# A longer planned landing for the two transfers of a range test, in a list-scheduled recurrence and FFN kernel

## The chip, the core and the metric

The kernel runs on one core of a Trainium2 chip. Its engines are TensorE (PE: matrix products, with its weight loads listed as PEld), VectorE (DVE), ScalarE (ACT), GpSimd (POOL) and SyncE (SP, which here does nothing but issue DMA transfers). Each engine works through its own list of instructions, and semaphores order one engine against another. The metric is the device time of one execution in microseconds; the figure for a kernel is the median of several executions.

## The reference, cut to what matters

A gated linear recurrence (48 channels per head, 8 heads, 4 sequences of 768 steps) is followed by a multiplicative feed-forward network (FFN) on the 3072 resulting rows.

```python
# attention block: q, k, v, f_logit are (4, 8, 768, 48), fp32
f = 1.0 / (1.0 + np.exp(-f_logit))
for t in range(S):
    state = f[:, :, t, :, None] * state + einsum('bhd,bhe->bhde', k[:, :, t], v[:, :, t])
    y[:, :, t] = einsum('bhd,bhde->bhe', q[:, :, t], state)
x = y.transpose(0, 2, 1, 3).reshape(3072, 384)

# FFN: w1, w2 are (384, 1024), w3 is (1024, 1024), w_out is (1024, 384)
a = x @ w1
b = x @ w2
h = a * b @ w3
out = h @ w_out
```

## The kernel before: the parts that matter here

**Two paths and a test between them.** The recurrence is cut into 24 units of 128 steps (`u` = 0 to 23). A fast path (`ranged`) multiplies q by the running product of the gates and k by its inverse. This holds only while these running products stay within a range, so the kernel tests the range at run time; if it is left anywhere, a second path (`general`) computes everything anew. The fast path leaves a flag `left`, and the branch at the very end reads it. On these inputs the second path isn't entered in the profile.

The test needs the last unit's results. It has six small VectorE operations (`judge`), a transfer that writes 112 numbers from SBUF to a scratch buffer in HBM (`told`), a transfer that reads them back as one row of one partition (`heard`), and two more VectorE operations: the row's minimum and the comparison that makes the flag (`decided`).

```python
def judge():
    ...
    nc.vector.tensor_reduce(out=low, in_=lasts, axis=AX.XY, op=ALU.min)             # L1233
    nc.vector.tensor_scalar(zero, ysum, 0.0, None, ALU.mult)                        # L1235
    nc.vector.tensor_reduce(out=nil, in_=zero, axis=AX.X, op=ALU.add)               # L1237
    nc.vector.tensor_scalar(nil, nil, 0.0, None, ALU.is_equal)                      # L1238
    nc.vector.tensor_scalar(low, low, RANGE, None, ALU.is_ge)                       # L1240
    nc.vector.tensor_tensor(good, low, nil, ALU.mult)                               # L1241
def told():
    where["all"] = dram.tile([R, 1], F32, name="good")                              # R = 112
    nc.sync.dma_start(where["all"], where["good"])                                  # L1246
def heard():
    row = work.tile([1, R], F32, name="row")
    nc.sync.dma_start(row, where["all"].rearrange("r one -> one r"))                # L1250
def decided():
    nc.vector.tensor_reduce(out=least, in_=where["row"], axis=AX.X, op=ALU.min)     # L1255
    nc.vector.tensor_scalar(left, least, 0.5, None, ALU.is_lt)                      # L1256
```

**A plan makes the order.** The kernel isn't written in the order in which it is emitted. Every piece of work is a task with an engine, an assumed cost, the tasks it depends on and a priority. `Plan.order()` runs a small list scheduler in Python when the kernel is built: it takes, again and again, the task that can start first by the assumed costs, and the tasks are then emitted in the order of their assumed start. The assumed costs are thus nowhere in the program; only the order on each engine comes from them. A transfer is two tasks, an issue on SP and a task on an engine called "DMA", whose `lag` is the time that a dependent task on another engine must keep from its end:

```python
def after(t, ds):                         # when may task t start, with the tasks ds before it
    return max([0.0] + [d["end"] + (d["lag"] + t["slack"] if d["eng"] != t["eng"] else 0.0) for d in ds])

def moves(n, size, rate, emit, deps, prio, late=0.0):
    for j in range(n):
        i = plan.add("SP", 0.45, (lambda: None) if j else emit, [d] if j else deps, prio - j * 1e-3, takes=["lane"], lag=0.6)
        d = i
        t = plan.add("DMA", size / n / rate, lambda: None, [i], prio - j * 1e-3, lag=1.3 + late, frees=[i])
    return t
```

**The FFN of a block of 512 rows.** Each of the six blocks (`n` = 0 to 5) has two stages. The first makes `a * b` (the tile `ab`); the second, `down(i)`, multiplies it by `wc`, which is w3 @ w_out folded into one matrix. Except in parts of the first two blocks' first stage, both stages use a scheme of 7 products in place of 8, which needs sums ahead of the products and after them. `down` runs twice for each block; its products on PE and its sums on VectorE are as follows (X, Y and Z are PSUM banks, all named `f` in the profile):

```python
m1 : X  = ab(0,0) wc         # PE, L714     k1 : dns["m1"] = X            # ACT, L959
m6 : Y  = abs_[1] wct        # PE, L714     u2 : dns["u2"] = Y + m1       # DVE, L965
m2 : X += ab(0,1) wc         # PE, L714     c11: o1 = X                   # ACT, L972
m7 : Y += abs_[2] wct        # PE, L714     u3 : dns["u3"] = Y + m1       # DVE, L978
m5 : Z  = abs_[0] wct        # PE, L714     c22: o2 = Z + u3              # DVE, L989
m4 : Y += ab(1,1) wct        # PE, L714     c21: o2 = Y + m1              # DVE, L995
m3 : Z += abs_[3] wc         # PE, L714     c12: o1 = Z + u2              # DVE, L1003
S0 to S3: the sums abs_[0] to abs_[3] of parts of ab                      # DVE, L950
...
pe("m7", m7, [q["u2"], q["S2"]], -3)
dve("u3", 0.36, u3, [q["m7"]] + old("c22"))
pe("m4", m4, [q["u3"]], -4)
...
pe("m3", m3, [q["c22"], q["S3"], q["m4"]] + ([judged] if final else []), -4)
```

`u3` reads the bank Y before `m4` adds to it, so `m4` must wait for `u3`. Only the last `down` of the last block needs the test's outcome (`judged`). Each of these matmuls in the source shows as two MATMUL instructions in the profile, so each of m1 to m7 is 8 of them. The first stage of a block uses lines L817 to L856, its sums of x L784; the output rows are stored by L1008, two stores for each `down`.

**Where the test is put in:**

```python
if u == NU - 1:
    looked = plan.add("DVE", 1.0, judge, [tk[i]["y"] for i in range(NU)], -20)
    sent = moves(1, 0.4, 250, told, [looked], 0)
    judged = plan.add("DVE", 0.2, decided, [moves(1, 0.4, 250, heard, [sent], 0)], -20)
```

Of the kernel before, what the change touches and what calls it, by code (L numbers as in the profile page):

```python
# [152 lines left out]
@with_exitstack  # L153
def kernel(
    ctx: ExitStack,
    tc: tile.TileContext,
    q: bass.AP,
    k: bass.AP,
    f_logit: bass.AP,
    v: bass.AP,  # L160
    w1: bass.AP,
    w2: bass.AP,
    w3: bass.AP,
    w_out: bass.AP,
    leaf_mask: bass.AP,
    out: bass.AP,
):
    nc = tc.nc
    const = ctx.enter_context(tc.tile_pool(name="const", bufs=1))
    ident = const.tile([P, P], F32, name="ident")  # L170
    w12 = const.tile([P, 2, KM, DFF], F32, name="w12")
    wc = const.tile([P, KF, DM], F32, name="wc")
    left = const.tile([1, 1], I32, name="left")
    with tc.manual_schedule():
        outside = ranged(tc, q, k, f_logit, v, w1, w2, w3, w_out, out, ident, w12, wc, left)
        with tc.If(outside > 0, preferred_fallthrough_block=True, label="general"):
            general(tc, q, k, f_logit, v, leaf_mask, out, ident, w12, wc)
# [29 lines left out]
def ranged(ctx, tc, q, k, f_logit, v, w1, w2, w3, w_out, out, ident, w12, wc, left):  # L207
# [53 lines left out]
    plan = Plan()  # L261
# [71 lines left out]
# [8 lines that stand above are left out]
# [231 lines left out]
    def together(u):  # L572
        return u >= LOOSE

    def begin(u):

        def emit():
            pairs(u)
            if u % NCH < NCH - 1:
                turn(u)  # L580

        t = tk[u]
        t["a"] = t["t"] = plan.add(
            "PE", 1.5, emit, [t["q"], t["k"]] + past(u, 1, "m", "d", "y") + past(u, 2, "d"), need(u) - 999, slack=0.8,
        )
        paired(u)
# [672 lines left out]
    for u in range(NU):  # L1259
        if u <= NPE:  # L1260
            front(u)
        if u >= NPE:
            if not (u > NPE and together(u - 1)):
                begin(u)
            if u + 1 < NU:
                front(u + 1)
        rest(u)
        if u == NPE - 1:
            weights()
        if u == NU - 1:  # L1270
            looked = plan.add("DVE", 1.0, judge, [tk[i]["y"] for i in range(NU)], -20)
            sent = moves(1, 0.4, 250, told, [looked], 0)
            judged = plan.add("DVE", 0.2, decided, [moves(1, 0.4, 250, heard, [sent], 0)], -20)
        if u % UB == UB - 1:
            ffn(u // UB)
    ready_at = 0.0
# [346 lines left out]
```

## Time and profile before

| what | value |
|---|---|
| time, median of 3 executions (lowest, highest) | 495.4 us (494.01, 496.9) |
| time of the profiled execution, its span | 496.72 us, 495.0 us |
| mean granted TensorE clock over the span | 0.993 of full speed |
| PE busy | 481.2 us |
| VectorE busy | 360.3 us |
| transfer of the 112 numbers to HBM (issue to landing) | 6.2 us |

Times in a profile are counted from the start of its span, in us. "Busy" adds up the instructions of an engine. The clock row of a page gives the clock that TensorE was granted, in tenths of full speed, for each of 40 slices of 12.4 us. A line of the timeline has start, duration, engine, source line, operation, the tiles written and read (out<-in), shapes and the number of merged instructions; what stands in square brackets is how long the engine had been idle before and what ended it. PE's matmuls overlap in their pipeline, so the time that one costs in a dense run is the distance from start to start, and not its duration.

### The profile page before, as it was taken

How to read it: one execution, taken by the hardware profiler on the slowest of the kernel's cores; microseconds unless marked ns; L12 is line 12 of the kernel's file. 1: busy time of each engine (PE TensorE's matmuls, PEld its weight loads, DVE VectorE, ACT ScalarE, POOL GpSimd, SP SyncE). 2: the span in 40 equal slices, each digit the busy share in tenths (PEclk: the TensorE clock that was granted, in tenths of full speed). 3: DMA queues.
4: the chain of work that ended last, by engine and by line, in shares of the span. 5: the costliest groups of instructions: out<-in, count | busy, mean ns of one | idle time of the engine just before them, and what ended most of it. 6: DMA issues, size and time to landing. Idle time of an engine off the chain costs nothing.

```text
span 495.0 us, 9560 instructions
## 1 busy us (share of the span) xinstructions
PE 481.2 (97%) x3696; PEld 411.4 (83%) x3696; DVE 360.3 (73%) x721; ACT 166.1 (34%) x380; POOL 61.6 (12%) x115
## 2 busy tenths in 40 slices
PE   8899999999999999999999999899999999999995
PEld 6788645666799888899888888898899888889994
DVE  7999899989997688698968864256673667664541
ACT  4688446663343553436244431010100111110010
POOL 9210000313211121123211210000000000000000
PEclk9999999999999999999999999799999999999999
DMA  6889476653336563455632111000021000000011
GB/s 175 298 304 267 123 260 246 197 168 81 84 98 176 143 150 91 112 132 153 181 80 53 33 52 47 32 33 0 2 64 49 16 1 0 1 1 0 33 59 45
DMA packets 44920, 50.00 MB, mean 101 GB/s; under 512 B 15426, under 2 KB 34370, under 8 KB 43842
## 3 DMA queue, kind: packets, MB, share of 16 engines
q1 hardware_dynamic: 44866, 49.30, 34.0%
q8 instruction: 31, 0.51, 0.4%
q14 instruction: 23, 0.19, 0.1%
HBM read 40.63 MB, written 8.65 MB: 100 GB/s over the span
## 4 chain that ended last, share of the span: by engine, by line
PE 82%; DVE 7%; DMA 3%; issue 1%; SPq 0%; DVEq 0%
PE f L714 67%; PE f L1176 4%; PE py L490 4%; PE pa L456 2%; PE py L509 2%; PE py L468 2%; DVE place L1208 1%; DMA good<-good 1%; PE f L523 1%; DMA xt<-yt 1%; DVE place L1123 1%; DVE place L1129 1%; DVE bwd L415 1%; PE f L692 1%; DMA row<-good 1%
## 5 line engine op out<-in xcount | busy, mean ns | idle before, releaser
L714 PE MATMUL f<-xt,w 128*128 128x256 f32 (+1 forms) x600 | 159.0, 396 | 0.0
L714 PEld LDWEIGHTS f<-xt,w 128*128 128x128 f32 x600 | 113.5, 190 | 24.7 <-issue 10.8
L714 PE MATMUL f<-place 128*128 128x192 f32 (+1 forms) x504 | 112.1, 350 | 0.4 <-DVE place L950 0.4
L714 PEld LDWEIGHTS f<-place 128*128 128x128 f32 x504 | 87.8, 190 | 6.4 <-DVE place L950 0.7
L549 POOL TENSOR_SCALAR_AFFINE_SELECT A<-A 64x256 f32<-64x256 f32 (+1 forms) x84 | 49.2, 606 | 231.9 <-PE py L468 105.9
L1176 PE MATMUL f<-place 128*128 128x384 f32 x128 | 42.6, 489 | 0.5 <-DVE place L1129 0.5
L817 ACT COPY a<-f 128x256 f32<-128x256 f32 x36 | 13.4, 373 | 81.4 <-PE f L714 69.4
L1176 PEld LDWEIGHTS f<-place 128*128 128x128 f32 x128 | 23.9, 190 | 17.3 <-DVE place L1129 1.1
L714 PE MATMUL f<-xt,place 128*128 128x256 f32 x144 | 37.1, 380 | 0.0
L714 PE MATMUL f<-wc,ab 128*128 128x192 f32 x192 | 35.4, 328 | 0.0
L714 PEld LDWEIGHTS f<-wc,ab 128*128 128x128 f32 x192 | 32.5, 192 | 0.4
L393 DVE TENSOR_TENSOR_SCAN fwd<-gate,floor 112x512 f32<-112x512 f32 x24 | 29.9, 1244 | 2.5 <-ACT gate L385 2.0
L543 ACT COPY A<-pa 64x256 f32<-64x256 f32 (+1 forms) x60 | 24.3, 439 | 20.2 <-PE pa L456 19.6
L415 DVE TENSOR_TENSOR_SCAN bwd<-gate,back 112x512 f32<-112x512 f32 x24 | 29.6, 1232 | 0.7
L714 PEld LDWEIGHTS f<-xt,place 128*128 128x128 f32 x144 | 26.6, 189 | 3.5 <-issue 0.2
L841 DVE TENSOR_TENSOR place<-f,a 128x256 f32<-128x256 f32 x36 | 15.2, 421 | 18.7 <-PE f L714 18.5
L653 ACT COPY sb<-S 48x192 f32<-48x192 f32 x40 | 14.0, 350 | 27.7 <-DVE S L644 18.2
L490 PEld LDWEIGHTS py<-A,vt 128*64 128x64 f32 (+1 forms) x320 | 17.5, 129 | 6.7 <-issue 6.2
L1112 ACT ACTIVATE place<-place 128x512 f32<-128x512 f32 (+2 forms) x24 | 21.4, 893 | 4.0 <-DVE w L1129 2.0
L714 PE MATMUL f<-place,ab 128*128 128x192 f32 x96 | 19.2, 346 | 3.6 <-DVE place L978 3.6
L490 PE MATMUL py<-A,vt 128*64 128x128 f32 x320 | 22.6, 281 | 0.0
L1115 ACT ACTIVATE place<-place 128x512 f32<-128x512 uint32 (+2 forms) x24 | 21.4, 900 | 0.9 <-DMA place<-in_w_out_dram 0.9
(119 smaller groups left out, 641.8 us busy)
## 6 DMA issues: line engine op xcount, KB each, us to landing
place<-in_w_dram SPq DMA_DIRECT2D x8, 1024.0 KB, 4.9
place<-in_w_dram SPq DMA_DIRECT2D x12, 512.0 KB, 9.9
out_dram<-o SPq DMA_DIRECT2D x24, 192.0 KB, 1.9
q<-in_q_dram SPq DMA_DIRECT2D x46, 96.0 KB, 2.5
f<-in_f_logit_dram SPq DMA_DIRECT2D x44, 96.0 KB, 2.4
k<-in_k_dram SPq DMA_DIRECT2D x44, 96.0 KB, 2.3
yt<-ys SPq DMA_DIRECT2D x40, 96.0 KB, 2.1
xt<-yt SPq DMA_DIRECT2D x20, 192.0 KB, 2.7
```

The lines of the kernel that those rows point to most:

```text
L393: nc.vector.tensor_tensor_scan(s["P"], gate[u % 2][:, 0:NQ], floor, 0.0, ALU.mult, ALU.max)
L415: nc.vector.tensor_tensor_scan(s["R"][:, ::-1], gate[u % 2][:, NQ:0:-1], back[:, ::-1], 0.0, ALU.mult, ALU.max)
L490: nc.tensor.matmul(y_block(u, b)[64 * half : 64 * half + w], lhsT=s["v"][:, h * D : h * D + w], rhs=s["A"][:, par, hp], start=zone not in ...
L543: nc.scalar.copy(parts_of(s["A"].rearrange("p r h c -> p (r h c)"))[p0:p1, :, f], parts_of(s["pa"].rearrange("p r n -> p (r n)"))[p0:p1, : ...
L549: nc.gpsimd.affine_select(out=a, in_=a, pattern=pattern, compare_op=ALU.is_ge, fill=0.0, base=0, channel_multiplier=-1,)
L653: nc.scalar.copy(sb[u % 2][rows(par), :, 64 * par : 64 * par + D], s["S"][rows(par)])
L714: nc.tensor.matmul(out_, lhsT=lhs[i], rhs=rhs[i], start=start and i == 0, stop=i == len(lhs) - 1, skip_group_check=True,)
L817: nc.scalar.copy(q["a"], q["X"])
L841: nc.vector.tensor_tensor(ups["u3", k], q["Y"], q["a"], ALU.add)
L1112: nc.scalar.activation(m, hi.bitcast(F32), AF.Abs)
L1115: nc.scalar.activation(lo.bitcast(F32), lo, AF.Copy, bias=2.0, scale=2.0**-51)
L1176: nc.tensor.matmul(w3s["p", jc], lhsT=w3s[jc][:, kc * P : kc * P + P], rhs=wos[:, kc], start=(kc == 0), stop=(kc == KF - 1),)
```

## The change

The two transfers of the test get a further argument, `late` = 20.0. In the plan, a task that depends on either of them on another engine must now keep 21.3 us from its end in place of 1.3. No operation is added or taken away, and no dependency is changed; what changes is the place of the minimum in VectorE's order (behind sums of the FFN that stood behind it), and the place of the second transfer in SP's.

```diff
         if u == NU - 1:
             looked = plan.add("DVE", 1.0, judge, [tk[i]["y"] for i in range(NU)], -20)
-            sent = moves(1, 0.4, 250, told, [looked], 0)
-            judged = plan.add("DVE", 0.2, decided, [moves(1, 0.4, 250, heard, [sent], 0)], -20)
+            sent = moves(1, 0.4, 250, told, [looked], 0, 20.0)
+            judged = plan.add("DVE", 0.2, decided, [moves(1, 0.4, 250, heard, [sent], 0, 20.0)], -20)
```

## The prediction

> **What bounds the kernel now.** I read the page first: the engines' totals and the clock row.
>
> ```profile
> PE 481.2 (97%) x3696; PEld 411.4 (83%) x3696; DVE 360.3 (73%) x721; ACT 166.1 (34%) x380; POOL 61.6 (12%) x115
> ...
> PEclk9999999999999999999999999799999999999999
> ```
>
> PE is busy for 97% of the span, so nearly everything that another engine does is hidden, and only what makes PE stand still, or run slower, counts. The clock row has one bad slice, the 26th, which covers 309.4 to 321.8 us. That is where the test of the range stands. So I went to the chain that ended last, in order of time, around that place:
>
> ```profile
> 301.84 6.17 DMA good<-good
> 308.02 2.61 DMA row<-good
> ...
> 311.40 174.77 PE f L714 x890
> ```
>
> The chain is PE nearly all the way, but here it leaves PE for 9 us and goes through the test's two transfers. From 311.40 on it is matmuls without a break for 174.77 us, so whatever PE gains before 311.40 should reach the end whole. The timeline of these microseconds shows how a test that nobody needs before the end of the kernel gets into PE's way:
>
> ```profile
> 305.65 0.69 DVE L950 TENSOR_TENSOR place<-ab 128x512 f32<-128x512 f32 x1 [0.94 <-PE f L714]
> 306.38 0.69 DVE L950 TENSOR_TENSOR place<-place,ab 128x512 f32<-128x512 f32 x1
> ...
> 306.75 1.46 PE L714 MATMUL f<-wc,ab 128*128 128x192 f32 x8
> 308.02 0.28 SPq L1250 DMA_DIRECT2D row<-good  x1
> 310.65 0.26 DVE L1255 TENSOR_REDUCE least<-row 1x1 f32<-1x112 f32 x1 [3.58 <-DMA row<-good]
> 310.94 0.14 DVE L1256 TENSOR_SCALAR left<-least 1x1 int32<-1x1 f32 x1
> 311.01 0.34 DVE L978 TENSOR_TENSOR place<-f,place 128x192 f32<-128x192 f32 x1
> ...
> 311.40 2.92 PE L714 MATMUL f<-place,ab 128*128 128x192 f32 x8 [3.19 <-DVE place L978]
> ```
>
> VectorE finishes two sums at 307.07 and then stands for 3.58 us in front of the minimum, because the row is still in flight. Behind the minimum stands u3 (L978), which has nothing to do with the test; PE's m4 waits for u3 and starts at 311.40. The windows of the trace (PE, PEld, DVE, ACT and POOL busy, then granted clock, DMA share, GB/s) show a second cost, in the clock column:
>
> ```profile
> 311.40:313.00 1.60, 1.60 (x5) 1.60 (x6) 0.94 (x2) 0.00 (x0) 0.00 (x0) 0.50 0.02 5
> ...
> 316.00:317.00 1.00, 1.00 (x4) 1.00 (x4) 0.07 (x1) 0.00 (x0) 0.00 (x0) 0.50 0.18 63
> 317.00:318.00 1.00, 1.00 (x7) 1.00 (x7) 0.88 (x2) 0.00 (x0) 0.00 (x0) 0.86 0.00 0
> ```
>
> After the pause PE runs at half clock until about 317.3: some 4 matmuls to the microsecond, where there are 7 or 8 later. To size it I took the same three groups of products (m4, m3, and m2 of the other half) once here and once at the last `down`, where the clock is full:
>
> ```profile
> 316.68 1.76 PE L714 MATMUL f<-wc,ab 128*128 128x192 f32 x8
> ...
> 318.28 4.06 PE L714 MATMUL f<-place 128*128 128x192 f32 x24
> ```
>
> ```profile
> 478.19 1.46 PE L714 MATMUL f<-place,ab 128*128 128x192 f32 x8
> ...
> 482.09 4.06 PE L714 MATMUL f<-place 128*128 128x192 f32 x24
> ```
>
> From the start of m4 to the start of the next products it is 318.28 - 311.40 = 6.88 us here and 482.09 - 478.19 = 3.90 us there, for the same 24 matmuls.
>
> **What the Trainium skill says.** "TensorE: Matmul & The Clock Gate", its opening table: VectorE's and ScalarE's queues are strictly first in, first out. The trace agrees: u3's bank was complete at about 306.9, VectorE sat idle, and u3 still ran only after the minimum. The same page, Part 1 (The HAM clock gate): after an idle window of about 3.4 us the array's clock is halved, and it takes a busy window to bring it back; the windows run freely, so the outcome depends on how a pause falls on them. The trace agrees: a pause of 3.19 us, then a clock of 0.50 for about 6 us. "Perfetto Trace Analysis", DMA Instruction — HWDGE: the final semaphore write waits until the data is written, which can take surprisingly long when the target is HBM. Here 0.4 KB to HBM took 6.17 us. "DMA: Bandwidth & Descriptors", Rules for kernel authors: issue the transfer early, and wait on its semaphore late. That is this change.
>
> **The change part by part.** The order of instructions of both kernels, engine by engine, differs in two places only. On VectorE the minimum and the comparison leave their place ahead of u3 and go 53 instructions further back, into the first stage of the next block, behind an L838. On SP the second transfer goes behind the four stores of this block's two `down`s. PE's, ScalarE's and GpSimd's orders stay.
>
> *The gap.* The 8 matmuls at 306.75 take 1.30 us start to start at full clock (as 478.19 to 479.49 for a group of 8), so m4 could start at 306.75 + 1.30 = 308.05. It starts at 311.40. With the minimum gone, u3 needs the end of m7 (302.85 + 4.06 = 306.91 in the timeline) and of VectorE's sum before it (306.38 + 0.69 = 307.07); it takes 0.34, so it ends at about 307.45, 0.6 us ahead of need. The gap goes whole: 311.40 - 308.05 = **3.35 us**.
>
> *The clock.* Without a pause there is no reason for the clock to fall: 6.88 - 3.90 = **2.98 us**.
>
> *What follows directly.* m3 needs c22 (L989, right after u3, done at about 307.85), and m2 of the other half needs k1, which needs c21. At the last `down` the same chain runs at full clock: c21 (L995) starts at 479.69, k1 ends at 480.46, m2 starts at 480.79. So 0.3 us stay free, and no wait replaces the one removed.
>
> *The minimum's new place.* The fourth store waits for an L1003 that now ends at 327.93, and 6.3 us earlier after the change, at 321.6. The second transfer goes out behind that store: 0.34 + 0.28 us for the two issues, and 2.6 us to land, as now; it is there at about 325. The L838 ahead of the new place ends at 353.10 now, at about 346.8 then: the row has some 22 us to spare. The two operations take 0.26 + 0.14 us, about 0.43 with the spaces between, and VectorE is idle there for 0.37 us. They stick out by 0.06 us beside a PE that doesn't wait at that place: 0.
>
> *SP.* The stores no longer stand behind a transfer that waits for another; the next gathers of x (L687) come at 358.6 and wait for PE. 0.
>
> *Sum.* 3.35 + 2.98 = **6.33 us**, all on the path: 1.3% of the span.
>
> **The rivals.**
>
> *The clock's dip isn't the pause's.* If it comes from something else, only the gap goes: 3.35 us, 492 to 493 us. For it: 3.19 us is less than the page's window. Against it: over the rest of the trace the windows show full clock, and the dip begins inside this pause.
>
> *A wait takes its place.* u3 could wait for something else, or the minimum could wait again further back and hold an L852 behind it. The first would leave a part of the 3.35, as at the last `down` (0.45 us of PE's waiting for L978; there no other matmuls stand between m7 and m4, as they do here). The second needs a row over 20 us late. About 490.5 to 491 for the first, 495 for the second.
>
> *The end is set elsewhere.* If the last block waited for its x or for a store, the gain would be given back, and the time would stay at 495. Against it: 174.77 us of unbroken PE, and x of the last block is gathered at 358 to 362 for use beyond that.
>
> *The profiled execution isn't the typical one.* Its 496.72 us is near the top of the three (494.01 to 496.9). The spread of 2.9 us is about as large as the clock's part; and how far the clock falls should depend on where the pause falls in the windows, as should the gap on the write to HBM. Then the median execution has less to lose than 6.33 us. I take this to be partly so.
>
> **From these to the time.** Working from the profiled execution: 496.72 - 6.33 = 490.4. From the median with the whole loss: 495.4 - 6.33 = 489.1. From the median with half the clock's part: 495.4 - 3.35 - 1.5 = 490.55. I choose **490.2 us**, 1.05% less. For 8 in 10 I take 488.6 to 491.8: the low end is the median with the whole loss and 0.5 us of luck, the high end lets most of the clock's part stay or be absent in the typical execution. A gain of over 2% would need 485.5 us, 9.9 us off where the trace holds 6.3: 0.02. Slower by 2% needs a new wait of 10 us, and none is in sight: 0.01.
>
> **What would show it.** In the changed kernel's timeline: u3 (L978) in the middle of this stage right behind the second of the two L950, no wait of PE for it of over 0.1 us, and start to start 3.90 us, not 6.88, for the next 24 matmuls; no 7 in the clock row; L1255 some 35 to 40 us further back than the test's first part, without a wait for the row; the times of executions closer together than 2.9 us. Wrong would be: a dip of the clock without the pause, a PE wait near the minimum's new place, or a stage after 318 us that takes longer than before.

## The result, and the profile after

The changed kernel takes **490.3 us** (median of 4 executions, 489.99 to 490.37) against 495.24 us before (median of 4, 494.01 to 496.9): a ratio of 0.9897, 95% interval 0.9867 to 0.9926. The profiled execution takes 490.37 us with a span of 488.7; before it was 496.72 and 495.0.

The same two rows of the page, engines and granted clock:

```profile
PE 477.4 (98%) x3696; PEld 408.0 (83%) x3696; DVE 359.8 (74%) x721; ACT 166.2 (34%) x380; POOL 61.5 (13%) x115
...
PEclk9999999999999999999999999999999999999999
```

The instruction counts are those of before, and VectorE has lost nothing of its work. The 7 in the clock row is gone. The chain that ended last, around the place where it went through the test's two transfers:

```profile
298.20 1.06 PE py L490 x14
299.26 0.58 PE py L509 x16
299.84 30.26 PE f L714 x165
```

Here it doesn't leave PE any more. The timeline of the same stage, with the two sums on VectorE, PE's group ahead of m4, u3, m4, m3 and the next products:

```profile
305.70 0.69 DVE L950 TENSOR_TENSOR place<-ab 128x512 f32<-128x512 f32 x1 [0.94 <-PE f L714]
306.43 0.69 DVE L950 TENSOR_TENSOR place<-place,ab 128x512 f32<-128x512 f32 x1
...
306.80 1.46 PE L714 MATMUL f<-wc,ab 128*128 128x192 f32 x8
307.04 0.35 DVE L978 TENSOR_TENSOR place<-f,place 128x192 f32<-128x192 f32 x1
...
308.10 1.46 PE L714 MATMUL f<-place,ab 128*128 128x192 f32 x8
309.40 1.46 PE L714 MATMUL f<-wc,place 128*128 128x192 f32 x8
...
312.00 4.06 PE L714 MATMUL f<-place 128*128 128x192 f32 x24
```

u3 (L978) follows the sums at once, and m4 starts at 308.10 with no idle time in brackets. From m4 to the next products it is 312.00 - 308.10 = 3.90 us, at full clock. The test's remains stand further back in the timeline:

```profile
322.14 0.30 SPq L1250 DMA_DIRECT2D row<-good  x1
...
346.40 0.42 DVE L838 TENSOR_TENSOR place<-f,a 128x256 f32<-128x256 f32 x1
346.74 0.25 DVE L1255 TENSOR_REDUCE least<-row 1x1 f32<-1x112 f32 x1
347.02 0.14 DVE L1256 TENSOR_SCALAR left<-least 1x1 int32<-1x1 f32 x1
347.19 0.42 DVE L852 TENSOR_TENSOR ab<-f,a 128x256 f32<-128x256 f32 x1
```

The minimum has no bracket: its row has long landed. And the first transfer was no faster than before: 7.2 us to HBM, where it had been 6.2. It is hidden, not shortened.

### The profile page after: what moved, and what is told of

The parts are those of the page before. It is cut to its first block, busy times and chain, and to the rows that moved or that the text cites. A ratio compares the mean times of both kernels' runs of the same rounds, so it can differ in the third digit from the quotient of the medians.

```text
span 488.7 us, 9559 instructions
## 1 busy us (share of the span) xinstructions
PE 477.4 (98%) x3696; PEld 408.0 (83%) x3696; DVE 359.8 (74%) x721; ACT 166.2 (34%) x380; POOL 61.5 (13%) x115
## 4 chain that ended last, share of the span: by engine, by line
PE 86%; DVE 6%; issue 1%; DVEq 0%
PE f L714 69%; PE f L1176 4%; PE py L490 4%; PE pa L456 2%; PE py L509 2%; PE py L468 2%; DVE place L1208 1%; PE f L523 1%; DVE place L1123 1%; DVE place L1129 1%; DVE bwd L415 1%; PE f L692 1%; DVE fwd L393 1%; DVE place L1222 0%; DVE place L950 0%
## 5 line engine op out<-in xcount | busy, mean ns | idle before, releaser
L1112 ACT ACTIVATE place<-place 128x512 f32<-128x512 f32 (+2 forms) x24 | 21.3, 886 | 4.0 <-DVE w L1129 2.0
L714 PE MATMUL f<-place,w 128*128 128x256 f32 x72 | 21.4, 379 | 0.0
L1115 ACT ACTIVATE place<-place 128x512 f32<-128x512 uint32 (+2 forms) x24 | 21.3, 893 | 0.0
```

The source lines that it names most:

```text
L714: nc.tensor.matmul(out_, lhsT=lhs[i], rhs=rhs[i], start=start and i == 0, stop=i == len(lhs) - 1, skip_group_check=True,)
L1112: nc.scalar.activation(m, hi.bitcast(F32), AF.Abs)
L1115: nc.scalar.activation(lo.bitcast(F32), lo, AF.Copy, bias=2.0, scale=2.0**-51)
```

## The experiments

The theory: VectorE works its queue in order, so a minimum whose row is in flight holds up u3, u3 holds up PE's m4, and PE's pause lowers its clock for the work that follows. The rivals: a part of the gain comes from SP's order; the dip of the clock has another cause; the minimum costs wherever it stands.

**Only the second transfer gets the 20 us.** This leaves SP's order as it was and moves only VectorE's two operations (by 23 instructions; the expectation below says 22).

```diff
-    judged = plan.add("DVE", 0.2, decided, [moves(1, 0.4, 250, heard, [sent], 0)], -20)
+    judged = plan.add("DVE", 0.2, decided, [moves(1, 0.4, 250, heard, [sent], 0, 20.0)], -20)
```

> Only the second transfer (the row's way back) gets the 20 us; the first keeps 1.3. VectorE's minimum then stands 22 instructions further back, and SP's order is that of the kernel before: the row's transfer ahead of the four stores. Theory (only VectorE's place of the minimum counts): 490.3 us within 0.5, no wait of PE for L978 in this stage. Rival (a part of the gain comes from SP, whose stores no longer stand behind a transfer that waits for another): between 491 and 494 us.

Measured: 490.34 us (4 executions, 490.12 to 490.40), ratio to before 0.9927 (0.9900 to 0.9954), and no wait of PE for L978 in this stage. All of the gain is there without SP's new order, so SP has no measurable part in it.

**A step of a few instructions: 1 us.** The edit is that of the run above with 1.0 in place of 20.0. The minimum then stands behind u3, c22 and a sum, ahead of c21.

> The second transfer gets 1.0 us in place of 20. VectorE's minimum then stands behind u3, c22 and one sum, ahead of c21. Theory (a queue in order stands still at the minimum until the row lands, whatever comes behind it): u3 runs at 307.1 and m4 follows without a gap, but c21 has to wait for the row (310.65 in the profile before) plus 0.4 us for the minimum and the comparison; it ends about 311.45 in place of 309.96, k1 about 311.85, and PE waits some 1.2 us ahead of m2 of the other half. The pause is too short to lower the clock: 491.5 us, or up to 492.5 us when the row is a microsecond later. Rival (any step out of u3's way gives all of the gain): 490.3 us. Rival (the wait as such costs, wherever it stands): 495 us.

Measured: 491.14 us (8 executions, 489.83 to 491.77, seven of them above 490.8), ratio 0.9938 (0.9919 to 0.9957). The timeline shows the same standstill one step further on:

```profile
310.40 0.26 DVE L1255 TENSOR_REDUCE least<-row 1x1 f32<-1x112 f32 x1 [2.13 <-DMA row<-good]
...
311.19 0.32 ACT L959 COPY place<-f 128x192 f32<-128x192 f32 x1 [7.87 <-DVE o L995]
...
311.56 1.57 PE L714 MATMUL f<-wc,ab 128*128 128x192 f32 x8 [0.80 <-ACT place L959]
```

VectorE stands 2.13 us in front of the minimum, c21 (L995) waits behind it, ScalarE's k1 (L959) for c21, and PE 0.80 us for k1. The chain is the expected one; its end is 0.3 us earlier than estimated (k1 done at 311.51, not 311.85). A stall of VectorE of 2.13 us makes PE wait for only 0.80 us, because m4 and m3 lie ahead of what it holds up.

**4 us, five instructions back.** Again the same edit, with 4.0: the minimum stands behind c12 (L1003).

> The second transfer gets 4.0 us. The minimum then stands behind u3, c22, a sum, c21 and c12 of the same half: 5 instructions further back than before, where the change puts it 53 further back. Theory (it is enough that the row has landed when VectorE gets to the minimum, or that nothing urgent stands behind it): c12 ends at about 311.3, the row lands at about 310.5, the sum and u2 behind it are needed by PE only at 313 or later: 490.3 us within 0.3. Rival (only a long way back is safe, since the landing varies by a microsecond or two): a median of 490.5 to 491.5 with executions above 491.

```profile
310.86 0.36 DVE L1003 TENSOR_TENSOR o<-f,place 128x192 f32<-128x192 f32 x1 [0.94 <-PE f L714]
311.13 0.25 DVE L1255 TENSOR_REDUCE least<-row 1x1 f32<-1x112 f32 x1
```

Measured: 490.34 us (4 executions, 490.20 to 490.38), ratio 0.9910 (0.9879 to 0.9940). The row has landed by 311.13, the minimum doesn't wait, and five instructions give all that 53 give.

**One transfer inside SBUF, at the old place in the plan.** The numbers go straight from a column over 112 partitions into a row of one partition.

```diff
+def crossed():
+    row = work.tile([1, R], F32, name="row")
+    nc.sync.dma_start(row, where["good"])
+    where["row"] = row
...
-    sent = moves(1, 0.4, 250, told, [looked], 0)
-    judged = plan.add("DVE", 0.2, decided, [moves(1, 0.4, 250, heard, [sent], 0)], -20)
+    judged = plan.add("DVE", 0.2, decided, [moves(1, 0.4, 250, crossed, [looked], 0)], -20)
```

> The plan of the kernel before, but the test's numbers go from one column over 112 partitions to one row of one partition in one transfer inside SBUF, without the scratch buffer in HBM and without the second transfer. The minimum keeps its old place ahead of u3. Theory (the landing of two chained transfers over HBM, 8.8 us, is what VectorE waits for): one transfer inside SBUF lands in about 2 to 2.6 us, at about 304.3, before VectorE gets to the minimum at 307.07; minimum and comparison take 0.43 us, u3 ends at about 307.9, ahead of the 308.05 at which m4 may start: 490.3 to 490.5 us. Rival (the place ahead of u3 is itself costly): over 492 us. Rival (112 elements of 4 bytes are slow wherever they go, 6 us): the row at 308, a gap of about 0.9 us on PE, 491.2 us.

The lines of the timeline: the last operation ahead of the minimum, and the minimum itself.

```profile
304.27 0.36 DVE L965 TENSOR_TENSOR place<-f,place 128x192 f32<-128x192 f32 x1 [1.84 <-PE f L714]
304.54 0.25 DVE L1260 TENSOR_REDUCE least<-row 1x1 f32<-1x112 f32 x1
```

Measured: 490.25 us (4 executions, 490.19 to 490.29), ratio 0.9926 (0.9899 to 0.9954). The transfer lands 1.9 us after its issue. With one transfer in place of two the plan put the minimum two instructions earlier than I had said, ahead of the two sums, and it still doesn't wait there. So an early place costs nothing by itself; what cost was the row in flight. It is also a second way to the same time: the answer comes sooner, where the change has VectorE ask for it later.

**PE kept busy in the pause: first at the wrong place.** To part the clock from the gap, seven matmuls into a bank that nobody reads were put on PE ahead of an m4 (14 MATMUL instructions in the profile). The first try chose a later block:

```diff
 def m4():
+    if n == NB - 2 and i == 0:
+        spare = ps.tile([P, 2, NQ], F32, name="pa")[:, 0, 0:TH]
+        for _ in range(7):
+            nc.tensor.matmul(spare, lhsT=floor[:, 0:P], rhs=floor[:, 0:TH], start=True, stop=True)
     three(q["Y"], each(quarter_(1, 1)), each(wct[3]), False)
```

> The kernel before, with 7 extra matmuls (128x256, into a bank that nobody reads) put on PE just ahead of the m4 that waits; VectorE's order and the test stay. Theory (the pause itself lowers the clock): the fill takes 7 x 0.43 = 3.0 us of a pause of 3.35 us, so PE never stands still for long, the clock stays at 1.00, and only the gap's 3.35 us remain: 490.3 + 3.35 = 493.6 us, and the 24 matmuls from m4 on take 3.90 us. Rival (the dip has another cause than the pause, for instance the work that follows): half clock as before, 6.9 us for the 24 matmuls, 495 to 496.5 us. Rival (the dip is rare and the gap alone is what the change won): same time as the kernel before, with the clock at 1.00 in both.

Measured: 496.07 us (8 executions, 495.48 to 498.18), ratio 1.0049 (1.0027 to 1.0071). The extra matmuls ran at 455 to 458 us, where PE waits for nothing, so they could not fill the pause, and the measured time doesn't bear on the question. (Two of the 8 executions have a mean clock of 0.996 or less, against 11 of the 17 of the kernel before beside them; 8 are too few to tell this from chance.) But the profiled execution caught a short wait:

```profile
309.22 0.26 DVE L1259 TENSOR_REDUCE least<-row 1x1 f32<-1x112 f32 x1 [2.24 <-DMA row<-good]
...
309.97 1.57 PE L714 MATMUL f<-place,ab 128*128 128x192 f32 x8 [1.85 <-DVE place L978]
```

The windows around it (PE, PEld, DVE, ACT and POOL busy, granted clock, DMA share, GB/s):

```profile
308.00:310.00 2.00, 0.15 (x2) 0.03 (x1) 0.71 (x4) 0.00 (x0) 0.00 (x0) 1.00 0.00 0
310.00:312.00 2.00, 2.00 (x12) 2.00 (x13) 1.26 (x3) 0.00 (x0) 0.00 (x0) 1.00 0.02 4
312.00:314.00 2.00, 2.00 (x15) 2.00 (x14) 0.95 (x2) 0.32 (x1) 0.00 (x0) 1.00 0.27 98
```

The row came 1.2 us after its issue, where it took 2.6 us in the profile before. PE paused for 1.85 us, the clock stays at 1.00, and the span of 493.7 us is the changed kernel's 488.7 plus 3.0 for the fill and 2.0 for the gap (309.97 - 306.66, less the 1.30 us of the group ahead, which starts at 306.66).

**PE kept busy in the pause: at the right place** (`n == 2 and i == 0` in the edit above).

> The kernel before with the 7 extra matmuls on PE ahead of the m4 that waits in this very stage (the fill before stood in the same place of the next block's work, where nothing waits). Theory (the pause lowers the clock): of a pause of 3.35 us in PE's work the fill takes 3.0, so the clock stays at 1.00 in every execution and the 24 matmuls from m4 on take 3.90 us. Executions with a long wait for the row come to 490.3 + 3.35 = 493.65 us; those with a short one pay the fill instead, 490.3 + 3.0 = 493.3 us. So all between 493.1 and 494.0, and no execution with a mean clock under 0.998, where the kernel before has a lower group at 492.2 to 493.7 (clock 0.998 to 1.000) and an upper one at 494.3 to 495.4 (0.995 to 0.996). Rival (the dip comes from what follows, not from the pause): about two in three executions at a mean clock of 0.995, and 495 us.

```profile
306.83 1.46 PE L714 MATMUL f<-wc,ab 128*128 128x192 f32 x8
308.13 3.19 PE L995 MATMUL pa<-floor 112*128 112x256 f32 x14
...
311.01 0.26 DVE L1259 TENSOR_REDUCE least<-row 1x1 f32<-1x112 f32 x1 [3.86 <-DMA row<-good]
...
311.76 1.57 PE L714 MATMUL f<-place,ab 128*128 128x192 f32 x8 [0.44 <-DVE place L978]
...
314.47 1.46 PE L714 MATMUL f<-wc,ab 128*128 128x192 f32 x8
```

The windows of this run, in the same columns:

```profile
310.00:312.00 2.00, 1.56 (x8) 1.05 (x7) 0.92 (x4) 0.00 (x0) 0.00 (x0) 1.00 0.00 0
312.00:314.00 2.00, 2.00 (x14) 2.00 (x14) 1.06 (x3) 0.18 (x1) 0.00 (x0) 1.00 0.02 4
```

VectorE's wait is even longer than in the profile before (3.86 us), and m4 starts at 311.76, later than its 311.40. But the clock stays at 1.00. m4 and m3 take 314.47 - 311.76 = 2.71 us for their 16 matmuls, where the kernel before needed 316.68 - 311.40 = 5.28 us. Measured: 493.59 us (22 executions, 493.0 to 494.59), ratio 0.9975 (0.9965 to 0.9986): work that nobody needs made the kernel before slightly faster, by the clock, since it doesn't shorten the gap. The mean clocks of the 22 executions are 0.997 to 1.000, as in the runs where the test holds up nothing, while 30 of the 37 executions of the kernel before that stand beside them have 0.996 or less. My limit of 0.998 was too tight, and so was the upper end of 494.0: the profiled execution (494.29 us) has the row later than I assumed.

**The minimum near the end: by 150 us in the plan.** The edit is that of the second transfer alone, with 150.0.

> The second transfer gets 150 us: the minimum stands among the last sums of the kernel, between u3 and c22 of the last half. Theory (a minimum whose row has landed costs 0.43 us of VectorE and only there): c22 ends 0.43 us later, at about 481.1, m3 starts at 481.7 in the changed kernel, so nothing waits: 490.3 us within 0.3. Rival (the end is tight, and what stands on VectorE there delays the end one for one, or the branch waits for the flag): 490.7 to 492 us.

Measured: 492.97 us (14 executions, 492.45 to 493.02 but for one in a slower state of the chip, at a mean clock of 0.947, with 508.03), ratio 0.9960 (0.9946 to 0.9974), 2.7 us above the changed kernel. My expectation was wrong, also on the place: the minimum stood at 417 us, among the sums of another block's `down`. PE's waits after 300 us:

```profile
PE f L714 <- DVE place L950: 2.0, 2, 1.0
```

PE waits for sums (L950), not for the test: 1.0 us at 410.66, before the minimum's place, and 1.0 us at 468.48. The orders show why: the plan moved PE's products as well. The two `down`s of the block before the last ran at 450 to 472 us in the kernel before, and begin at 408 us here, mixed with the first stage of the last block. By the plan's code, a transfer holds one of 8 lanes until its landing, and the lag counts there too; the eighth transfer behind the row is the fourth gather of x for the last block, and it alone was put off, behind four more stores. So the number doesn't act on the minimum alone: it also holds a lane in the plan. That the lane is the way from the number to the moved products is read from the code and the orders; no run changed the lanes alone.

**The minimum near the end, with the plan untouched.** To part the two, the plan of the kernel before was kept, and only the minimum and the comparison were moved behind the last u3:

```diff
-for t in plan.order():
+todo = [t for t in plan.order() if t is not judged]
+todo.insert([t is downq[-1]["c22"] for t in todo].index(True), judged)
+for t in todo:
```

> The plan of the kernel before, untouched; after planning, the minimum and the comparison are taken out of the order and put in again between u3 and c22 of the very last half, as far back as c22 allows. Only these two instructions change place, PE's and SP's orders are those of before. Theory (the 2.7 us that the 150 us cost came from the other work that the plan moved with them, 11 groups of PE's products among it, not from where the minimum stood): 490.3 us within 0.3; PE's waits after 300 us are the 0.4 us for L978 alone. Rival (a minimum near the end costs, by its 0.43 us of VectorE or because the branch then reads its flag late): 490.8 to 493 us.

```profile
480.06 0.25 DVE L1255 TENSOR_REDUCE least<-row 1x1 f32<-1x112 f32 x1
...
480.34 0.14 DVE L1256 TENSOR_SCALAR left<-least 1x1 int32<-1x1 f32 x1
480.41 0.34 DVE L989 TENSOR_TENSOR o<-f,place 128x192 f32<-128x192 f32 x1
...
481.60 1.46 PE L714 MATMUL f<-wc,place 128*128 128x192 f32 x8
```

Measured: 490.19 us (4 executions, 490.10 to 490.57), ratio 0.9902 (0.9872 to 0.9933). c22 (L989) ends 0.85 us before m3 needs it. A minimum 8 us before the end of the span costs nothing; the 2.7 us belong to the work that moved along with it, some 2.0 us of them to the two waits for sums. The rest was not taken apart. (The expectation counts 11 moved groups; the orders differ in more, all 14 groups of the two `down`s among them.)

**The versions.** 490.19, 490.25, 490.3, 490.34 and 490.34 us: the five ways of keeping VectorE out of the wait can't be told apart, and none beats the change.

**How much of it is clock.** Beside the experiments stand 61 executions of the kernel before, each with its mean clock. They fall into three groups:

| mean clock | executions | mean time | above 490.3 |
|---|---|---|---|
| 0.998 to 1.000 | 14 | 493.12 us | 2.8 us |
| 0.995 to 0.996 | 40 | 495.06 us | 4.8 us |
| 0.990 to 0.993 | 7 | 496.15 us | 5.9 us |

By its mean clock the first group pays the gap only. For the second, a rough estimate: a mean clock that is lower by 0.003 over some 493 us is 0.003 x 493 / 0.5 = 3 us at half clock, by which some 1.5 us are lost; the group is 1.9 us slower than the first. The runs without a dip have mean clocks of 0.997 to 1.000 themselves, so the 0.003 is uncertain by about as much, and the gap varies too (2.0 us in the profile of the first fill, 3.35 before): the table doesn't part the two exactly. The profiled execution before, with its 0.993, belongs to the third group. The changed kernel has no such pause, and its four times lie within 0.4 us.

## Why the prediction was right

Predicted 490.2 us, measured 490.3; a ratio of 0.9895 against 0.9897. The mechanism is the predicted one, part by part. That the time is met to 0.1 us is in part luck: 490.2 was chosen among estimates of 489.1, 490.4 and 490.55.

- **The gap.** Predicted 3.35 us. m4 now starts 1.30 us after the group ahead of it, which is what was counted on (306.80 to 308.10). u3 ends at 307.39, 0.7 us ahead of need; 0.6 was predicted.
- **The clock.** Predicted 2.98 us for the 24 matmuls; they now take 3.90 us in place of 6.88, as predicted. That the pause is the cause was an inference then; the filled pause, with the same 16 matmuls behind it at full clock, shows it.
- **The sum for the profiled execution.** Predicted 6.33 us; the profiled times differ by 496.72 - 490.37 = 6.35 us.
- **No new wait.** Predicted for u3, c22 and k1. PE's only wait for L978 is the 0.4 us at the very end, which was there before. The row goes out at 322.1 (predicted: behind a store at 321.6), the minimum runs at 346.74 (predicted: about 346.8), without a wait.
- **SP.** Predicted 0; the run with SP's order unchanged has the same time.
- **The typical execution.** That the profiled one loses more than the median one was the rival that I took to be partly so. It is: by their mean clocks, most executions lose about half as much to the clock as the profiled one did. Without this the median would have been put at 495.4 - 6.33 = 489.1, 1.2 us too low.
- **Two slips.** The prediction takes the change for a transfer issued early and waited for late. Only the waiting is later: the second transfer itself goes out 14 us later too (322.14 against 308.02), and it has time enough all the same. And I wrote that the minimum would come 35 to 40 us behind the test's first part. It comes 346.7 - 300.6 = 46 us behind; my own 346.8 said so already.

## What to carry to other kernels

In an engine that works in order, an operation that waits for a transfer must stand where its answer has arrived, or where nothing urgent stands behind it: nobody needed this test before the end, and it still held up the engine that bounds the kernel. Look for the cost of such a wait not only in the gap but also in the clock of the microseconds behind it, and compare the same work at another place of the trace, start to start. When a schedule is steered by an assumed latency, compare the orders afterwards: a small number did here all that a large one did, and a very large one moved work that had nothing to do with it.

## What the runs showed of the hardware

The first transfer, 112 numbers of 4 bytes to HBM, took 6.2 to 7.7 us from issue to landing in the nine profiles that have it, while the 96 KB writes to HBM (L684) took 2.1 us in the median; the same numbers sent across partitions inside SBUF took 1.9 us. Two of those 96 KB writes go out just ahead of it. In these nine profiles one of the two lands after 2.0 to 2.1 us, the other after 6.2 to 8.5 us; in the run with the transfer inside SBUF they take 2.0 and 2.5 us. So the writes ahead aren't slow by themselves: a large one becomes slow where the small transfer to HBM follows it. Why, and whether the small elements or something else makes that transfer slow, was not tried.

"TensorE: Matmul & The Clock Gate", Part 1, of the Trainium skill says that the windows that decide on the clock run freely, so that the same kernel can fare differently from run to run. Here the same program has a lowered mean clock (0.990 to 0.996) in 47 of 61 executions. How much of that comes from where the windows fall, and how much from a row that lands sooner or later, is not shown. In the profiles, pauses of PE of 0.80 and 1.85 us left the clock at full, and the one of 3.19 us didn't; nothing between was caught.
